# Attention memory of a fused attention and MLP-mixer kernel divided into pools by time of last use, and the main channel weights laid as a pool each on what falls free first

## The chip, the cores and the metric

The kernel runs on one core of a Trainium2 chip. The metric is the device time of one execution in microseconds (us); lower is better. TensorE (PE) does the matrix products, ScalarE (ACT) the exponentials, casts and copies, VectorE (DVE) the elementwise work, GpSimd (POOL) part of the subtractions, and SyncE (SP) issues all DMAs. Each of these takes its instructions in a fixed order.

## What is computed

Four batches, eight heads, 576 rows, head dimension 64. First linear attention with 256 exponential features, then two mixer blocks:

```python
def phi(x):
    proj = np.einsum('bhsd,df->bhsf', x, w_phi)
    proj = proj - np.max(np.abs(proj), axis=-1, keepdims=True)
    return np.concatenate([np.exp(proj), np.exp(-proj)], axis=-1)
kv = np.einsum('bhsf,bhsd->bhfd', k_p, v);  z = np.sum(k_p, axis=2)
num / (q_p . z + 1e-06)                     # attention
...
h = xt @ U @ V;  u = x + h.transpose(0, 2, 1)          # first block, rank 32 over the 576 tokens
u + np.maximum(u @ w_ch1, 0.0) @ w_ch2                 # 512 -> 2048 -> 512
...
h = np.maximum(xt @ w_tok1, 0.0) @ w_tok2;  u = x + h.transpose(0, 2, 1)   # second block, 576 -> 256 -> 576
u + np.maximum(u @ w_ch1, 0.0) @ w_ch2                 # 512 -> 1536 -> 512
```

The weights of the mixers are float64.

## The kernel before

**Products.** Every fp32 product is made of three products in the chip's rounded fp32 type: each operand is split into a high part (a cast) and a low part (value minus high part), and hi·hi, hi·lo and lo·hi are added in PSUM. So a tile of weights exists twice, as `wh` and `wl`.

**Stages.** Phase A is the attention, in 16 groups `g` of two heads, five rounds each, four groups for a batch. Into its rounds are woven, for each batch, the token mix of the first mixer (`tm0`, `tm1`, `tm2`: tiles `xp`, `xh`, `xl`, `rp`, `rh`, `rl`, `mp`) and the first 5 of the 16 column tiles of its channel MLP (`ma_u`, `ma_h`, `ma_y`: tiles `uha`, `hp_a`, `hha`, `hla`, `yp`). The "a" weights of these five live in the pool `wring`. Phase B does the other 11 column tiles, b0 to b10, and the token mix of the second mixer (`hp_b`, `hhb`, `hlb`, `yb`, `gp`). Phase C is the second channel MLP. The partial result of phase A goes to DRAM (`sD`, `uD`) and comes back in phase B (`x`, `ub`).

**Weights.** They come as raw float64 bits. `load64` brings half a tile, 512 KB, into a buffer `raw`. ACT makes `w` and `r` of it (lines 138, 139), DVE puts them together with two SCALAR_TENSOR_TENSOR (lines 141, 144; "the STTs"), then `wh` is cast on ACT and `wl` made on POOL. A tile has two halves, `_0` and `_1`: so `w_b1_0` is the first half of tile b1. There are two `raw` buffers in the pool `stage`, and in phase B three more in `rawx`. Which one a half gets is settled by a running count (`halves`) that isn't reset between the phases, and stands at 13 where phase B begins: so b0_0, b0_1 and b2_0 go to `rawx`, and b1_0, b1_1 to `stage`.

**Memory.** Pools `a1`, `a2`, `at2`, `ac` hold phase A. They are closed, and the pools of phase B (`wrB` for the seven tiles b0 to b6, then `rawx`, `bc`, `b2`) are laid on the same bytes; each tile there waits for the last use of the tiles that it lies on. b7 to b10 are in `wring` and wait for the "a" weights. PSUM likewise: `psy` takes banks 0 to 3, `psh` banks 4 and 5, `psg` banks 6 and 7, on the banks that `psk` (1), `psx` (5) and `psm` (2) had in phase A.

**Order.** The kernel is written as a list of rounds, but a scheduler with a time model then sets the order of instructions on each engine; `bufs`, pools and waits enter there. That order is fixed in the program. The end of phase A is one chain: numerators of group 15 are copied (`nd`), their denominators collected by DMA (`pk`), inverted, spread by two DMAs (`rD`, `rec`), multiplied (`xT`), and then the last batch's `tm0` to `ma_y` runs (all with the number 3: `xp3`, `rp3`, `hp_a3`, `yp3`).

Of the kernel before, what the change touches and what calls it, by code (L numbers as in the profile page):

```python
# [75 lines left out]
O_MA = 8  # L76
# [11 lines left out]
def body(ctx, tc, kq, vd, w_phi, U, V, wm1, wt1, wt2, wm2, out):  # L88
# [105 lines left out]
    warm = a1.tile([P, 512], F32R, tag="kvT", name="warm")  # L194
# [4 lines left out]
    wpr = a1.tile([P, F], F32, tag="wpr", name="wpr")  # L199
# [38 lines left out]
    def load(g):  # L238
        b, hp = g // NPAIR, g % NPAIR
        for i in range(NT):  # L240
            raws[g, i] = a1.tile([P, 2 * P], F32, tag="kq", name=f"kq{g}_{i}", bufs=KQB)
# [470 lines left out]
```

## Time and profile before

| | |
|---|---|
| median of three runs | 1089.06 us (1086.58 to 1089.66) |
| the profiled execution | 1084.32 us |
| its span, first to last instruction | 1082.5 us |
| around the span (difference) | 1.8 us |
| mean granted clock of TensorE in it | 0.984 |
| PE busy | 1038.5 us (96%) |
| DVE, ACT, POOL busy | 579.9, 420.0, 225.2 us |

Times in the views are microseconds from the start of the span. "Idle before, <- releaser" tells how long an engine stood before an instruction and which instruction ended that. TensorE's clock has two levels, 2.4 GHz (granted clock 1.00) and 1.2 GHz; a granted clock between is a mean over a stretch. Engines work in order, so an instruction that waits holds up all that stands behind it on its engine. Phase A ends and phase B begins at about 421 us.

### The profile page before, as it was taken

The page shows a single profiled execution, that of the slowest core. Times are in us where ns is not written, and L with a number is a line of the kernel's source. Part 1 is how long each engine was busy: PE and PEld are TensorE (multiplying, and loading weights), DVE is VectorE, ACT ScalarE, POOL GpSimd, SP SyncE. Part 2 cuts the span into 40 slices and gives each one's busy share as a digit, 9 for nine tenths or more (in the row PEclk, how much of TensorE's full clock was granted, in tenths as well). Part 3 has the DMA queues.
Part 4 walks back from the last instruction along what each step waited for, and adds up shares of the span by engine and source line. Part 5 has one row for each costly group of instructions (what it writes and reads, how often), then busy time and mean ns, then how long its engine had stood idle before and what let it go on. Part 6 is the DMA issues. An engine that isn't in the chain of part 4 may idle for free.

```text
span 1082.5 us, 16491 instructions
## 1 busy us (share of the span) xinstructions
PE 1038.5 (96%) x6528; PEld 945.5 (87%) x6528; DVE 579.9 (54%) x973; ACT 420.0 (39%) x953; POOL 225.2 (21%) x174
## 2 busy tenths in 40 slices
PE   8988999899989897999999999999999999999998
PEld 6767899799879797999999999999898888888886
DVE  7888988998898498733223223339941121211211
ACT  6766666755565466522112112137621111110110
POOL 3316566545555134100000000003200000000000
PEclk9988999999999889999999999999999999999999
DMA  7542322232221387520200200216401020020101
GB/s 214 169 139 63 98 73 75 72 96 71 80 74 45 109 287 228 168 79 22 88 23 22 88 22 23 88 41 208 143 23 61 1 77 1 1 77 1 39 1 38
DMA packets 59612, 87.36 MB, mean 81 GB/s; under 512 B 14352, under 2 KB 46352, under 8 KB 59536
## 3 DMA queue, kind: packets, MB, share of 16 engines
q1 hardware_dynamic: 59536, 86.32, 25.1%
q8 instruction: 51, 0.84, 0.3%
q14 instruction: 25, 0.20, 0.1%
HBM read 67.27 MB, written 18.95 MB: 80 GB/s over the span
## 4 chain that ended last, share of the span: by engine, by line
PE 78%; DVE 10%; ACT 4%; DMA 4%; issue 3%; POOL 1%; SPq 0%; DVEq 0%; ACTq 0%; POOLq 0%
PE hp_c L106 14%; PE yc L106 14%; PE hp_b L106 11%; PE yb L106 11%; PE hp_a L106 4%; PE pp L106 3%; PE yp L106 3%; PE nm L106 3%; PE kvp L106 3%; PE gp L106 3%; PE m2p L106 2%; PE dT L354 1%; DVE w_b L141 1%; DMA raw_b<-in_wm_dram 1%; DVE w_b L144 1%
## 5 line engine op out<-in xcount | busy, mean ns | idle before, releaser
L180 DVE SCALAR_TENSOR_TENSOR hlc<-hp_c,hhc 128x504 fp32r<-128x504 f32 (+1 forms) x60 | 38.2, 637 | 225.3 <-ACT hhc L179 225.3
L179 ACT ACTIVATE hhc<-hp_c 128x504 fp32r<-128x504 f32 (+1 forms) x60 | 33.4, 556 | 247.4 <-PE hp_c L106 247.4
L180 DVE SCALAR_TENSOR_TENSOR hlb<-hp_b,hhb 128x288 fp32r<-128x288 f32 x88 | 40.0, 456 | 157.9 <-ACT hhb L179 157.9
L179 ACT ACTIVATE hhb<-hp_b 128x288 fp32r<-128x288 f32 x88 | 36.0, 409 | 197.8 <-PE hp_b L106 197.5
L106 PE MATMUL hp_b<-uhb,wh_b 128*128 128x288 f32 x352 | 103.9, 296 | 3.4 <-DVE xT L491 3.4
L106 PE MATMUL hp_b<-ulb,wh_b 128*128 128x288 f32 x352 | 104.0, 296 | 0.0
L106 PE MATMUL hp_b<-uhb,wl_b 128*128 128x288 f32 x352 | 104.0, 296 | 0.0
L106 PE MATMUL yb<-hlb,wh_b 128*128 128x288 f32 x352 | 97.5, 297 | 1.4 <-DVE hlb L180 1.3
L106 PE MATMUL yb<-hhb,wl_b 128*128 128x288 f32 x352 | 97.1, 295 | 0.0
L106 PE MATMUL hp_c<-ulc,wh_c 128*128 128x504 f32 (+1 forms) x240 | 89.1, 371 | 0.0
L106 PE MATMUL hp_c<-uhc,wl_c 128*128 128x504 f32 (+1 forms) x240 | 89.1, 371 | 0.0
L106 PE MATMUL hp_c<-uhc,wh_c 128*128 128x504 f32 (+1 forms) x240 | 88.5, 371 | 0.0
L106 PE MATMUL yc<-hlc,wh_c 128*128 128x504 f32 (+1 forms) x240 | 88.3, 371 | 0.0
L106 PE MATMUL yc<-hhc,wl_c 128*128 128x504 f32 (+1 forms) x240 | 88.1, 370 | 0.0
L99 POOL TENSOR_TENSOR wl_c<-w_c,wh_c 128x512 fp32r<-128x512 f32 x12 | 19.1, 1593 | 326.6 <-ACT wh_c L94 312.5
L99 POOL TENSOR_TENSOR qel<-qe,qeh 128x640 fp32r<-128x640 f32 (+1 forms) x48 | 71.6, 1504 | 25.7 <-ACT qeh L94 10.7
L106 PE MATMUL yc<-hhc,wh_c 128*128 128x504 f32 (+1 forms) x240 | 75.7, 371 | 0.0
L106 PEld LDWEIGHTS hp_b<-uhb,wh_b 128*128 128x128 f32 x352 | 66.0, 188 | 4.9 <-DVE xT L491 3.6
L106 PE MATMUL yb<-hhb,wh_b 128*128 128x288 f32 x352 | 67.7, 296 | 0.9 <-ACT hhb L179 0.9
L106 PEld LDWEIGHTS yb<-hlb,wh_b 128*128 128x128 f32 x352 | 66.1, 188 | 2.5 <-DVE hlb L180 2.4
L106 PEld LDWEIGHTS hp_b<-ulb,wh_b 128*128 128x128 f32 x352 | 66.3, 188 | 0.1
L106 PEld LDWEIGHTS yb<-hhb,wl_b 128*128 128x128 f32 x352 | 66.2, 188 | 0.0
(181 smaller groups left out, 2796.4 us busy)
## 6 DMA issues: line engine op xcount, KB each, us to landing
raw_c<-in_wm_dram SPq DMA_DIRECT2D x24, 512.0 KB, 4.5
raw_b<-in_wm_dram SPq DMA_DIRECT2D x22, 512.0 KB, 4.7
kq<-in_kq_dram SPq DMA_DIRECT2D x80, 128.0 KB, 2.2
raw_a<-in_wm_dram SPq DMA_DIRECT2D x10, 512.0 KB, 4.0
rec<-rD SPq DMA_DIRECT2D x32, 144.0 KB, 3.2
uD<-xT SPq DMA_DIRECT2D x8, 576.0 KB, 3.4
sD<-xT SPq DMA_DIRECT2D x8, 576.0 KB, 5.3
x<-sD SPq DMA_DIRECT2D x8, 576.0 KB, 5.1
```

What stands on the lines that cost most here:

```text
L99: return ENG[e].tensor_tensor(out=o, in0=a, in1=b, op=ALU.subtract)
L106: nc.tensor.matmul(o, l, r, start=start, stop=stop, skip_group_check=True)
L141: nc.vector.scalar_tensor_tensor(out=wi, in0=wi, scalar=3, in1=r, op0=ALU.logical_shift_left, op1=ALU.bitwise_or)
L144: nc.vector.scalar_tensor_tensor(out=wi, in0=top, scalar=-(2**31), in1=wi, op0=ALU.bitwise_and, op1=ALU.bitwise_or)
L179: nc.scalar.activation(hh, hp, AF.Relu)
L180: nc.vector.scalar_tensor_tensor(out=hl, in0=hp, scalar=0.0, in1=f32(hh), op0=ALU.max, op1=ALU.subtract)
L354: nc.tensor.transpose(tp[:, o : o + r], ds["q", g, t][:r, j, :], ident[:r, :r])
```

## The change

The pools `a1` and `a2` become five: `ax` (projection weights, inputs and their splits), `ak` (features of k), `ad` (`kvT`, `km`, `kd`), `aq` (`KH`, `KL`, features of q) and `an` (`nd`, `pk`, `rec`). The tags and numbers of buffers stay. `wrB` becomes seven pools of one tile each, and `rawx` stands between the second and the third of them, so that the tiles of phase B lie on other tiles of phase A than before. The count in `load64` starts anew at phase B, so that b0_0 and b0_1 go to `stage` and b1_0, b1_1, b2_0 to `rawx`. `psh` is opened ahead of `psy`: `psh` gets banks 0 and 1, `psy` 2 to 5. `O_MA` becomes a tuple of four eights, which gives the same rounds. The number and kind of instructions on each engine is the same.

```diff
-O_MA = 8
+O_MA = (8, 8, 8, 8)
...
-    halves, extra = [], []
+    halves, extra = [0], []
...
-        pool = stage if len(halves) % (RAWB + RAWX) < RAWB or not extra else extra[0]
-        halves.append(name)
+        pool = stage if halves[0] % (RAWB + RAWX) < RAWB or not extra else extra[0]
+        halves[0] += 1
...
-        a1 = A.enter_context(tc.tile_pool(name="a1", bufs=1))
-        a2 = A.enter_context(tc.tile_pool(name="a2", bufs=2))
+        ax = A.enter_context(tc.tile_pool(name="ax", bufs=1))
+        ak = A.enter_context(tc.tile_pool(name="ak", bufs=1))
+        ad = A.enter_context(tc.tile_pool(name="ad", bufs=1))
+        aq = A.enter_context(tc.tile_pool(name="aq", bufs=2))
+        an = A.enter_context(tc.tile_pool(name="an", bufs=1))
...
-        e = a2.tile([P, 2, 2, F], F32, tag="ke", name=f"ke{g}_{t}", bufs=KEB)
+        e = ak.tile([P, 2, 2, F], F32, tag="ke", name=f"ke{g}_{t}", bufs=KEB)
...
-            nds[g, j] = a1.tile([P, S], F32, tag=f"nd{j}", name=f"nd{g}_{j}")
+            nds[g, j] = an.tile([P, S], F32, tag=f"nd{j}", name=f"nd{g}_{j}")
...
-        wrB = ctx.enter_context(tc.tile_pool(name="wrB", bufs=NR, reuse_waits="tile"))
-        extra.append(ctx.enter_context(tc.tile_pool(name="rawx", bufs=RAWX, reuse_waits="tile")))
+        wrB = []
+        for f in range(NR):
+            wrB.append(ctx.enter_context(tc.tile_pool(name=f"wrB{f}", bufs=1, reuse_waits="tile")))
+            if f == 1:
+                extra.append(ctx.enter_context(tc.tile_pool(name="rawx", bufs=RAWX, reuse_waits="tile")))
+    halves[0] = 0
...
+    psh = ctx.enter_context(tc.tile_pool(name="psh", bufs=2, space=PSUM, reuse_waits="tile"))
     psy = ctx.enter_context(tc.tile_pool(name="psy", bufs=1, space=PSUM, reuse_waits="tile"))
-    psh = ctx.enter_context(tc.tile_pool(name="psh", bufs=2, space=PSUM, reuse_waits="tile"))
...
-    wB = [load_w(wrB if f < NR else wring, wm1, NA + f, f"b{f}") for f in range(nB)]
+    wB = [load_w(wrB[f] if f < NR else wring, wm1, NA + f, f"b{f}") for f in range(nB)]
```

What moves is the order on ACT, DVE, POOL and SP. Four instructions of tile b0's first load go into group 4's work near 75 us; the loads and conversions of b1 to b7 begin in the last group, g = 15, and no more behind it; and the order on PE shifts a little between 85 and 215 us and between 340 and 432 us. In the rows below the last number of a name counts instructions, and the numbers ahead of it are those of the tile.

On ACT, near 75 us, before and then after: `nd3` are the numerators of group 3, `keh4` features of group 4.

```order
L94 CAST keh4_0_910<-ke4_0_907 128x512
L94 COPY nd3_0_850<-nm3_0_0_847 128x320
L94 COPY nd3_1_855<-nm3_1_0_852 128x320
L94 CAST xgh5_0_1067<-kq5_0_872 128x256
L94 COPY nd3_0_850<-nm3_0_1_884 128x256
```

```order
L94 CAST keh4_0_919<-ke4_0_916 128x512
L138 ACTIVATE w_b0_0_5588<-raw_b0_0_5586 128x512
L139 ACTIVATE r_b0_0_5589<-raw_b0_0_5586 128x512
L94 COPY nd3_0_859<-nm3_0_0_856 128x320
L94 COPY nd3_1_864<-nm3_1_0_861 128x320
L94 CAST xgh5_0_1076<-kq5_0_881 128x256
L94 COPY nd3_0_859<-nm3_0_1_893 128x256
L139 ACTIVATE r_b0_1_5599<-raw_b0_1_5596 128x512
L138 ACTIVATE w_b0_1_5598<-raw_b0_1_5596 128x512
```

The two pairs that make b0's `w` and `r` now stand in front of and between group 3's copies.

On ACT, at the end of the last group (the `qe15` and `nd15` are that group's features of q and numerators, `hha2` the third batch's hidden layer, `xh3` the first step of the last token mix), before:

```order
L94 COPY nd15_0_4830<-nm15_0_1_4860 128x256
L94 COPY nd15_1_4839<-nm15_1_1_4868 128x256
L179 ACTIVATE hha2_1_3_5085<-hp_a2_1_3_5072 128x288
L179 ACTIVATE hha2_1_4_5136<-hp_a2_1_4_5123 128x288
L138 ACTIVATE w_b0_0_5558<-raw_b0_0_5556 128x512
L139 ACTIVATE r_b0_0_5559<-raw_b0_0_5556 128x512
L94 CAST xh3_0_4967<-xp3_0_4962 128x512
L138 ACTIVATE w_b0_1_5568<-raw_b0_1_5566 128x512
```

and after, from the first of these conversions on:

```order
L138 ACTIVATE w_b1_0_5610<-raw_b1_0_5608 128x512
L139 ACTIVATE r_b1_0_5611<-raw_b1_0_5608 128x512
L363 ACTIVATE qe15_1_1_4825<-dT15_1_1_4822 128x256
L364 ACTIVATE qe15_1_1_4825<-dT15_1_1_4822 128x256
L94 CAST qeh15_0_1_4818<-qe15_0_1_4815 128x2x256
L138 ACTIVATE w_b1_1_5620<-raw_b1_1_5618 128x512
L139 ACTIVATE r_b1_1_5621<-raw_b1_1_5618 128x512
L179 ACTIVATE hha2_1_1_5045<-hp_a2_1_1_5032 128x288
...
L138 ACTIVATE w_b2_0_5632<-raw_b2_0_5630 128x512
L179 ACTIVATE hha2_1_3_5094<-hp_a2_1_3_5081 128x288
L94 COPY nd15_1_4848<-nm15_1_1_4877 128x256
```

Conversions of b1 and b2 now stand between the last group's features and its last copy; before, the first one came behind all of them.

On DVE, at the collecting of the denominators (`pk15`), before:

```order
L180 SCALAR_TENSOR_TENSOR hla2_1_3_5086<-hp_a2_1_3_5072,hha2_1_3_5085 128x288
L395 TENSOR_SCALAR pk15_4910<-pk15_4910 128x9
L396 RECIPROCAL pk15_4910<-pk15_4910 128x9
L180 SCALAR_TENSOR_TENSOR hla2_1_4_5137<-hp_a2_1_4_5123,hha2_1_4_5136 128x288
L491 TENSOR_TENSOR xT2_2880<-yp2_1_0_5140,xT2_2880 128x288
```

and after:

```order
L398 TENSOR_SCALAR pk15_4919<-pk15_4919 128x9
L180 SCALAR_TENSOR_TENSOR hla2_1_4_5146<-hp_a2_1_4_5132,hha2_1_4_5145 128x288
L144 SCALAR_TENSOR_TENSOR w_b2_1_5642<-raw_b2_1_5640,w_b2_1_5642 128x512
L399 RECIPROCAL pk15_4919<-pk15_4919 128x9
L494 TENSOR_TENSOR xT2_2889<-yp2_1_0_5149,xT2_2889 128x288
```

Between the sum and the reciprocal there are now two more instructions.

On SP, at the same place, after the change (before, all loads of b tiles stood behind the two `rec15`):

```order
L391 DMA pk15_4919<-nd15_0_4839 64x1x9
L392 DMA pk15_4919<-nd15_1_4848 64x1x9
L133 DMA raw_b4_1_5684<-in_wm1_dram 128x512
L133 DMA raw_b5_0_5696<-in_wm1_dram 128x512
L401 DMA rD15_4941<-pk15_4919 128x9
L403 DMA rec15_4943<-rD15_4941 64x576
L404 DMA rec15_4943<-rD15_4941 64x576
L133 DMA raw_b5_1_5706<-in_wm1_dram 128x512
```

Two loads of weights stand ahead of the spreading of the reciprocals.

On DVE, at the end of phase A, before: `hla3` and `yp3` belong to the last batch.

```order
L144 SCALAR_TENSOR_TENSOR w_b7_0_5712<-raw_b7_0_5710,w_b7_0_5712 128x512
L99 TENSOR_TENSOR ulb0_1_6228<-ub0_1_6225,uhb0_1_6227 128x1152
L491 TENSOR_TENSOR xT3_4303<-yp3_1_0_5456,xT3_4303 128x288
L141 SCALAR_TENSOR_TENSOR w_b7_1_5722<-w_b7_1_5722,r_b7_1_5723 128x512
L491 TENSOR_TENSOR xT3_4303<-yp3_1_1_5473,xT3_4303 128x288
L144 SCALAR_TENSOR_TENSOR w_b7_1_5722<-raw_b7_1_5720,w_b7_1_5722 128x512
L491 TENSOR_TENSOR xT3_4303<-yp3_1_2_5490,xT3_4303 128x288
L491 TENSOR_TENSOR xT3_4303<-yp3_1_3_5507,xT3_4303 128x288
```

and after:

```order
L180 SCALAR_TENSOR_TENSOR hla3_1_4_5462<-hp_a3_1_4_5448,hha3_1_4_5461 128x288
L99 TENSOR_TENSOR ulb0_1_6258<-ub0_1_6255,uhb0_1_6257 128x1152
L494 TENSOR_TENSOR xT3_4312<-yp3_1_0_5465,xT3_4312 128x288
L494 TENSOR_TENSOR xT3_4312<-yp3_1_1_5482,xT3_4312 128x288
L494 TENSOR_TENSOR xT3_4312<-yp3_1_2_5499,xT3_4312 128x288
L494 TENSOR_TENSOR xT3_4312<-yp3_1_3_5516,xT3_4312 128x288
```

The conversions are gone from this place; they stand further ahead.

## Rows read from the trace of the kernel before

**Rows 1.** The page's first section: engine, busy us, share of the span, instructions.

```profile
PE 1038.5 (96%) x6528; PEld 945.5 (87%) x6528; DVE 579.9 (54%) x973; ACT 420.0 (39%) x953; POOL 225.2 (21%) x174
```

**Rows 2.** Busy time by stretch: us, length, PE, PEld, DVE, ACT, POOL, clock, DMA share, GB/s.

```profile
360.00:380.00 20.00, 15.43 (x77) 12.57 (x76) 12.21 (x21) 10.85 (x20) 3.21 (x3) 0.79 0.46 155
380.00:400.00 20.00, 19.29 (x128) 18.60 (x128) 18.29 (x27) 13.82 (x24) 7.39 (x7) 0.87 0.94 319
420.00:440.00 20.00, 14.96 (x109) 14.26 (x108) 15.41 (x20) 12.58 (x24) 8.27 (x7) 1.00 0.62 196
440.00:460.00 20.00, 19.95 (x150) 19.68 (x149) 14.52 (x36) 9.37 (x24) 2.57 (x2) 1.00 0.56 165
```

**Rows 3.** Waits of PE from 360 to 440: who for whom, total us, times, longest.

```profile
PE hp_b L106 <- DVE xT L491: 3.4, 1, 3.4
PE rp L106 <- ACT xh L94: 3.2, 1, 3.2
PE yp L106 <- DVE hla L180: 1.2, 2, 0.9
PE yb L106 <- DVE hlb L180: 1.2, 1, 1.2
PE yb L106 <- ACT hhb L179: 0.5, 1, 0.5
```

**Rows 4.** Timeline of PE: start, length, instruction, [idle before and releaser].

```profile
369.45 0.80 PE L106 MATMUL rp<-xh,US 128*128 128x512 f32 x1 [3.16 <-ACT xh L94]
...
383.88 0.61 PE L106 MATMUL hp_a<-uha,wh_a 128*128 128x288 f32 x1 [0.47 <-ACT uha L94]
...
424.42 0.40 PE L106 MATMUL hp_b<-uhb,wh_b 128*128 128x288 f32 x1 [3.41 <-DVE xT L491]
```

**Rows 5.** Timeline of DVE at three places.

```profile
359.58 0.17 DVE L395 TENSOR_SCALAR pk<-pk 128x9 f32<-128x9 f32 x1 [0.46 <-DMA pk<-nd]
...
364.37 1.54 DVE L411 TENSOR_TENSOR xT<-nd,rec 64x576 f32<-64x576 f32 x2 [2.07 <-DMA rec<-rD]
...
379.42 1.76 DVE L144 SCALAR_TENSOR_TENSOR w_b<-raw_b,w_b 128x512 int32<-128x512 int32 x1
381.11 2.27 DVE L445 TENSOR_TENSOR xT<-mp,xT 128x288 f32<-128x288 f32 x6
```

**Rows 6.** Timeline of ACT at six places.

```profile
74.61 0.43 ACT L94 COPY nd<-nm 128x320 f32<-128x320 f32 x1 [0.86 <-PE nm L106]
...
346.27 0.59 ACT L94 COPY kvT<-kvp 128x512 f32<-128x512 f32 x1 [0.60 <-PE kvp L106]
...
350.55 0.40 ACT L360 ACTIVATE qe<-dT 128x256 f32<-128x256 f32 x1
...
357.30 0.37 ACT L94 COPY nd<-nm 128x256 f32<-128x256 f32 x1 [0.74 <-PE nm L106]
...
367.71 0.66 ACT L138 ACTIVATE w_b<-raw_b 128x512 f32<-128x512 f32 x1 [7.48 <-DMA raw_b<-in_wm_dram]
...
368.82 0.58 ACT L94 CAST xh<-xp 128x512 fp32r<-128x512 f32 x1
```

**Rows 7.** Timeline of SP, its DMA issues, at two places.

```profile
70.64 3.65 SPq L133 DMA_DIRECT2D raw_b<-in_wm_dram  x2
...
361.97 0.59 SPq L401 DMA_DIRECT2D rec<-rD  x1
362.67 8.57 SPq L133 DMA_DIRECT2D raw_b<-in_wm_dram  x4
```

**Rows 8.** The page's DMA issues: operation, count, size, median us to landing.

```profile
raw_b<-in_wm_dram SPq DMA_DIRECT2D x22, 512.0 KB, 4.7
```

**Rows 9.** The STTs on raw_b from 340 to 440 us: shortest, median, longest ns.

```profile
L144 DVE SCALAR_TENSOR_TENSOR w_b<-raw_b,w_b x21: 675/692/1761, 370.2 to 439.0; 128x512 int32<-128x512 int32 x21
```

**Rows 10.** Loads of kq, 128 KB each, from 60 to 90 us.

```profile
DMA to landing us min/median/max: 2.0/2.3/4.0
```

**Rows 11.** Busy time from 60 to 120 us, the sum of three stretches.

```profile
sum 60.00, PE 50.07 PEld 41.50 DVE 50.67 ACT 39.65 POOL 29.41; mean PE 16.69 PEld 13.83 DVE 16.89 ACT 13.22 POOL 9.80
```

More of the change, by code (lines that the diff above doesn't have):

```diff
@@ L192, in body @@
     psm = PS.enter_context(tc.tile_pool(name="psm", bufs=PSMB, space=PSUM))
-    warm = a1.tile([P, 512], F32R, tag="kvT", name="warm")
+    warm = ad.tile([P, 512], F32R, tag="kvT", name="warm")
     nc.vector.memset(f32(warm), 0.0)
@@ L198, in body @@
         mm(wp, warm[:, :P], warm, i == 0, i == WARM - 1)
-    wpr = a1.tile([P, F], F32, tag="wpr", name="wpr")
+    wpr = ax.tile([P, F], F32, tag="wpr", name="wpr")
     nc.sync.dma_start(wpr[0:D], w_phi)
@@ L240, in load @@
         for i in range(NT):
-            raws[g, i] = a1.tile([P, 2 * P], F32, tag="kq", name=f"kq{g}_{i}", bufs=KQB)
+            raws[g, i] = ax.tile([P, 2 * P], F32, tag="kq", name=f"kq{g}_{i}", bufs=KQB)
             nc.sync.dma_start(raws[g, i], kq[b, hp, :, i])
@@ L250, in load_v @@
         else:
-            vrs[g] = a1.tile([P, NT, 2, D], F32, tag="vr", name=f"vr{g}")
+            vrs[g] = ax.tile([P, NT, 2, D], F32, tag="vr", name=f"vr{g}")
             nc.sync.dma_start(vrs[g], vd[b, hp])
@@ L256, in g_split @@
             return
-        xh = a1.tile([P, 2 * P], F32R, tag="xgh", name=f"xgh{g}_{i}", bufs=XGB)
-        xl = a1.tile([P, 2 * P], F32R, tag="xgl", name=f"xgl{g}_{i}", bufs=XGB)
+        xh = ax.tile([P, 2 * P], F32R, tag="xgh", name=f"xgh{g}_{i}", bufs=XGB)
+        xl = ax.tile([P, 2 * P], F32R, tag="xgl", name=f"xgl{g}_{i}", bufs=XGB)
         split(raws[g, i], xh, xl, "a", "v")
@@ L300, in k1 @@
             return
-        eh = a2.tile([P, 2, 2 * F], F32R, tag="keh", name=f"keh{g}_{t}", bufs=KHB)
+        eh = ak.tile([P, 2, 2 * F], F32R, tag="keh", name=f"keh{g}_{t}", bufs=KHB)
         cp(KHI[t], eh, ev)
         if t < 4:
-            el = a2.tile([P, 2, 2 * F], F32R, tag="kel", name=f"kel{g}_{t}", bufs=KHB)
+            el = ak.tile([P, 2, 2 * F], F32R, tag="kel", name=f"kel{g}_{t}", bufs=KHB)
             sub(KLO[t], el, ev, f32(eh))
@@ L329, in k3 @@
     def k3(g):
-        kvT = a1.tile([P, 2, 2 * F], F32, tag="kvT", name=f"kvT{g}")
+        kvT = ad.tile([P, 2, 2 * F], F32, tag="kvT", name=f"kvT{g}")
         cp("a", kvT, kvps.pop(g))
@@ L364, in q1 @@
             return
-        eh = a2.tile([P, 2, 320], F32R, tag="qeh", name=f"qeh{nm}", bufs=QHB)[:, :, :n]
-        el = a2.tile([P, 2, 320], F32R, tag="qel", name=f"qel{nm}", bufs=QHB)[:, :, :n]
+        eh = aq.tile([P, 2, 320], F32R, tag="qeh", name=f"qeh{nm}", bufs=QHB)[:, :, :n]
+        el = aq.tile([P, 2, 320], F32R, tag="qel", name=f"qel{nm}", bufs=QHB)[:, :, :n]
         split(e, eh, el, QHI[2 * ch + j], "p")
@@ L386, in x0 @@
     def x0(g):
-        pk = a2.tile([P, 9], F32, tag="pk", name=f"pk{g}")
+        pk = an.tile([P, 9], F32, tag="pk", bufs=2, name=f"pk{g}")
         nc.sync.dma_start(pk[0:D], nds[g, 0][D : D + 1, :])
@@ L398, in xr @@
         nc.sync.dma_start(rD.rearrange("a (p i) -> (a p) i", i=9), pk)
-        rec = a1.tile([P, S], F32, tag="rec", name=f"rec{g}", bufs=RECB)
+        rec = an.tile([P, S], F32, tag="rec", name=f"rec{g}", bufs=RECB)
         nc.sync.dma_start(rec[0:D], rD[0:1].to_broadcast([D, S]))
@@ L640, in body @@
     BX.close()
-    wC = [load_w(wrB if f < NR else wring, wm2, f, f"c{f}") for f in range(NF2)]
+    wC = [load_w(wrB[f] if f < NR else wring, wm2, f, f"c{f}") for f in range(NF2)]
     with tc.using_default_side("right"):
```

16 lines of the change are left out of this document (8 added, 8 removed).

## The prediction

> **What bounds the kernel now.** I read the page's busy times first: PE is busy 96% of the span [rows 1], so only time in which PE stands still, or runs slowly, can be won. Next I read the busy times by stretch, to find where that is. The stretch 440 to 460 is what a full one looks like: 150 matmuls, clock 1.00. Around the seam of phases A and B it is otherwise: 77 matmuls from 360 to 380 at clock 0.79, 128 from 380 to 400, 109 from 420 to 440 [rows 2]. Then the waits of PE in that region, which name the releasers: 3.4 us at the first `hp_b`, 3.2 us at `rp`, 1.2 at `yp`, 1.2 and 0.5 at `yb` [rows 3], 9.5 us together. The other loss there is the low clock on a chain of small steps, `rp3` (369.45) to `hp_a3` (383.88), 14.4 us long [rows 4]. The timelines tell why PE waits. DVE is busy 18.29 of 20 us from 380 to 400 [rows 2], and much of that are the STTs that put the weights b1 to b7 together. On ACT, `xh3` runs at 368.82 only, because a `w_b` stands ahead of it and waits for its DMA until 367.71 [rows 6]; that DMA was issued at 362.67, behind the last `rec` [rows 7].
>
> So the seam is where the change can act. It puts no instruction on PE and takes none away.
>
> **The change part by part.** The sum is made against the profiled execution, 1084.32 us (span 1082.5 and 1.8 around it). That one is 4.7 us under the median of 1089.06, so I carry the difference over to the median.
>
> *Two halves of b0 early, near 75 us.* The load that stood there, issued at 70.64 [rows 7], becomes b0's, and ACT now stands for it ahead of the copies of group 3. With the median of 4.7 us [rows 8] it lands at 75.3. ACT had nothing to do from 73.75 (74.61 less 0.86, [rows 6]). Two conversions of 0.66 [rows 6] follow, so the first copy ends its wait at 76.6 in place of 74.6, 2.0 us late. DVE gets four STTs of 0.69 to 1.76 [rows 9], 2.8 to 7 us. But of the 60 us around, DVE is busy 50.67 and PE 50.07 [rows 11]: neither is full, and group 3's copies are several rounds ahead of their use in `xT`. Ends: -1 (PE's order from 85 to 215 us moves a little, and may move well) and +4 (the 2.0 us and half of four slow STTs come through). I take +0.5, near zero, as both engines have air.
>
> *The seam, first part: the weights in the last group's way.* The loads of b1 may now start once the last features of k are used by the `kvp` products, whose copy began at 346.27 [rows 6]. An estimate from that row and from the median landing of 4.7 us [rows 8] puts the first load's landing at 351.3, with 0.3 for the issue. On ACT its two conversions, 1.3 us, stand ahead of a feature step that began at 350.55 [rows 6]: 2.0 us late. The next two conversions and a cast, ahead of the hidden layer and the last copies, add about 1.0 net: I take 3.0 us for the last copy of `nd15`, which began at 357.30 [rows 6]. Bounds 2.6 and 3.6. Behind this wait stand the casts of `qeh15` and the steps of `hha2`, and behind those PE's products; but these have the gap at 366 to run into, so only the chain to `xT3` counts. Next, between the sum of `pk15` (359.58, [rows 5]) and its reciprocal stand an `hla2` of 0.46 and an STT of 0.69 to 1.76 [rows 9]: 1.1 us, bounds 0.7 and 2.2. Next, `rD15` stands on SP behind two loads of 512 KB. The nearest row is `kq` behind a load, 4.0 us at most against 2.3 in the median [rows 10]: 1.7 us. Bounds 0, if the loads have gone, and 3.3, which is 1.05 MB at the 319 GB/s of the busiest stretch [rows 2]. So the `xT3` products, which ended at 365.91 (364.37 and 1.54, [rows 5]), come 5.8 us later.
>
> The Trainium skill (DMA: Bandwidth & Descriptors, section "Queues, rings and completion order") says that each DMA engine takes the descriptors of a queue in ring order, so that a small transfer waits for all bytes queued ahead of it. By that rule the upper bound of 3.3 holds and the sum comes out 1.6 us higher; the `kq` row agrees that it costs something, and no row here has a tiny transfer behind two loads.
>
> *The seam, second part: what is no more in the way.* With those products done, `xh3` needs no DMA any more: by the durations on PE and ACT it would have let `rp3` start at about 367.35, some 1.4 us behind `xT3` (four transposes of about 0.2 and a cast of 0.58, [rows 6]), and not at 369.45 [rows 4]. That is 2.1 us back. In the chain behind, an STT of 1.76 at 379.42 stands ahead of the sums into `xT3` at 381.11 [rows 5]; after the change none stands there: 1.6 us back. Other conversions, of b4 to b7, stand between the same steps, as b0 to b2 did; I count no difference. So `hp_a3` comes at 5.8 - 2.1 - 1.6 = +2.1 us. Bounds: 2.6 + 0.7 + 0 - 3.7 = -0.4 and 3.6 + 2.2 + 3.3 - 2.1 = +7.0.
>
> *The seam, third part: the waits up to 430 us.* From `hp_a3` to the first products of b0, DVE no longer has conversions between its steps. The two waits of `yp` for `hla` go: -1.2. The first `hp_b` waited 3.4 us for the last sum into `xT` [rows 3, 4], since its PSUM bank held the `yp3` of that sum. Its bank is now one that was free 70 us before, its weights b0 are made near 80 us, and its inputs are ready before `yp3` ends: -3.4. The wait of `yb` for `hlb`, 1.2, came from STTs of b8 and b9 ahead of it [rows 3]. The four of b8 stand there still, but their inputs are ready, so they run while PE does the first `hp_b`: -1.2. Of ACT's 0.5 I count a half. Together -6.0. Bounds -6.3 (all five rows but `rp`) and -4.6 (the first and the `hla` alone). What cover do these have? If b8 to b10 came late, PE would wait there again. At 150 matmuls in 20 us [rows 2] the 24 of a tile take 3.2 us, so PE reaches b10 some 32 us after the first `hp_b`, at 424.42 [rows 4]; the last of the 21 STTs listed began at 439.0 [rows 9], 14.6 us after it. There is room.
>
> *No cost:* the five pools of phase A hold the same tags with the same buffers; `O_MA` gives the same rounds; phase C has the same pools under other names.
>
> The sum: 0.5 + 2.1 - 6.0 = -3.4 us. On the profiled execution that is 1080.9, on the median 1085.6.
>
> **The rivals.** *A, the tail is held longer, and the kernel gets slower.* The chain from the first wait on ACT to `xT3` is made of three in-order queues, ACT, DVE and SP, each with a load or a conversion put ahead of the critical step. At its upper bounds (+7.0), with the early halves at +2 and the savings at -4.6, the result is +4.4: 1093.5. The point from which the change loses is `hp_a3` 5.5 us late, which is `xT3` about 9 us late, at 375. For it: everything on that chain is short, and a load in flight is long (4.7 us); the clock is low there anyway (0.79, [rows 2]), and more idle time won't raise it. Against it: the loads come in spread out by DVE's pace, not four at once. The ring rule above is part of this rival.
>
> *B, the tail isn't held.* The loads land before ACT needs them, and the last copies come less than a microsecond late. Then `hp_a3` comes 2 to 3 us earlier rather than later, and the waits go as well: 0 - 2.5 - 6.0 = -8.5, 1080.6. For it: at 360 to 380 the DMA engines are busy less than half of the time [rows 2]. Against it: 350.55 is only 4.3 us after the earliest issue that I see, and a load takes 4.7.
>
> *C, a new wait takes the place of the old at the seam.* b7 to b10 lie in `wring` and wait for `yp3` as before. If PE, starting 3.4 us earlier, caught up with them, the gain at `hp_b` would come back as a wait for `wh_b`; with the tail at +2.1 that is -3.4 + 3.4 = 0, 1089. Against it: the room of 17 us worked out above. That the change doesn't do what it says, in that the loads aren't earlier at all, I leave out: they stand earlier in the order and what they wait for ends earlier.
>
> **How the numbers follow.** About 0.3%, 3.3 us, is what a measurement of this kernel can tell from no change: 1085.8 to 1092.3 is "the same". My forecast (0.58) is -3.4, give or take 4, just about on that edge: half of it is faster, nearly half the same. B has 0.15 and is faster. A has 0.18, all but a little slower. C has 0.09, the same. That gives faster 0.44, same 0.37, slower 0.19. The range of 8 in 10 goes from 1079.5, a little beyond B, to 1093, nearly the price of A.
>
> **What would show it.** In the profile of the changed kernel: the wait of PE at the first `hp_b` gone and `hp_b` directly behind `yp3`; no waits of `yp` for `hla` from 400 on; ACT idle for a DMA at about 347 to 352 ahead of `w_b`; the `xT3` products ending near 372 and `hp_a3` starting near 386. I am wrong if the `xT3` products come beyond 375 (A), if they come at 367 or sooner (B), if PE waits for a `wh_b` of b7 to b10 (C), or if PE's waits from 60 to 220 us change by more than 4 us, which no step here accounts for.

## The result: slower by 0.7%

| | median | span of the runs | runs |
|---|---|---|---|
| before | 1087.30 us | 1081.27 to 1089.66 | 6 |
| changed | 1092.43 us | 1088.52 to 1096.46 | 6 |

The ratio is 1.0072 (95% interval 1.0051 to 1.0094), where 0.997 was forecast. (Three of the six runs of before are those that the prediction started from. Against the median of the other three, 1084.95 us, the changed kernel's median is 0.7% longer; against that of all six, 0.5%.) In a later set of runs on one chip (e11 below) the changed kernel stood at 1.0060 (1.0039 to 1.0080). The profiled execution of the changed kernel took 1091.15 us, with a span of 1089.4: 6.9 us over that of before.

**Where the time went.** I matched instructions by their names in the two programs and compared the start or end of the same one in both traces. "Late" means against the profiled execution of before.

| point in the program | before | changed | late |
|---|---|---|---|
| last `kvp` product of group 3 | 66.37 | 68.29 | +1.9 |
| last `kvp` product of group 10 | 225.28 | 233.86 | +8.6 |
| last `kvp` product of group 14 | 321.14 | 329.75 | +8.6 |
| first `rp3` | 369.45 | 383.53 | +14.1 |
| first `hp_a3` | 383.88 | 398.57 | +14.7 |
| last `yp3` | 421.01 | 433.44 | +12.4 |
| last product of the first `yb` | 463.84 | 470.74 | +6.9 |
| last product | 1077.88 | 1085.01 | +7.1 |

So there are three pieces. The attention loses 6.7 us between 66 and 225 us (the 1.9 ahead of that arise where no engine's order has changed). The way to `hp_a3` loses another 6.1. From there to the end of the first `yb` 7.8 come back. The seam as a whole gains 1.7, and the early part loses four times that.

The waits of PE around the seam in the changed kernel: who waited for whom, total, times, longest.

```profile
PE xp L426 <- DVE xT L414: 6.3, 1, 6.3
PE rp L106 <- DVE xl L99: 1.2, 2, 1.0
PE hp_a L106 <- ACT uha L94: 1.1, 1, 1.1
PE mp L106 <- DVE rl L99: 0.9, 1, 0.9
PE mp L106 <- ACT rh L94: 0.7, 1, 0.7
PE yp L106 <- DVE hla L180: 0.7, 1, 0.7
PE rp L106 <- ACT xh L94: 0.7, 1, 0.7
...
PE yb L106 <- ACT hhb L179: 0.2, 1, 0.2
```

Against [rows 3] the 3.4 us at `hp_b` are gone, and so are those of `yp3` and of `yb` for `hlb`. The 3.2 us of `rp` for `xh` have become 0.7. But ahead of it stands a new wait, 6.3 us of `xp3` for the `xT3` products. (The 0.7 of `yp` for `hla` is at 370 us, in the third batch.)

The busy time by stretch, columns as in [rows 2]:

```profile
360.00:380.00 20.00, 15.34 (x114) 14.87 (x113) 15.46 (x25) 15.65 (x32) 10.40 (x8) 1.00 0.57 185
380.00:400.00 20.00, 12.99 (x54) 9.96 (x54) 18.17 (x28) 13.69 (x24) 7.09 (x5) 0.74 0.62 209
400.00:420.00 20.00, 19.73 (x148) 19.36 (x147) 13.16 (x19) 7.78 (x14) 2.90 (x2) 1.00 0.70 236
420.00:440.00 20.00, 19.75 (x147) 19.40 (x147) 9.77 (x16) 9.15 (x17) 5.50 (x4) 1.00 0.46 148
```

The stretch of the token mix is now 380 to 400, with 54 matmuls and a clock of 0.74; behind it PE is full, 148 and 147 matmuls, and DVE has air (13.16 and 9.77 of 20 us). That is what the change was laid out for; it stands behind a longer hole.

**The early piece.** On ACT at 75 us, in the changed kernel (start, length, instruction, idle before):

```profile
75.06 0.64 ACT L94 CAST keh<-ke 128x512 fp32r<-128x512 f32 x1
77.36 0.67 ACT L138 ACTIVATE w_b<-raw_b 128x512 f32<-128x512 f32 x1 [1.66 <-DMA raw_b<-in_wm_dram]
77.93 0.66 ACT L139 ACTIVATE r_b<-raw_b 128x512 int32<-128x512 uint32 x1
78.49 0.74 ACT L94 COPY nd<-nm 128x320 f32<-128x320 f32 x2
```

ACT stood 1.66 us for the load, as forecast, and the two copies of `nd3` came behind it. Both halves of b0 are converted here, with four instructions on ACT and four STTs on DVE, and once they are read two more loads of 512 KB go out, from 83.18 us on. (Up to 140 us no engine waits for a load of `kq`, which stands behind these two.) The busy time from 80 to 90 us of the changed kernel, and then that of the same work in before, which stands 1.9 us earlier there:

```profile
80.00:90.00 10.00, 7.52 (x52) 6.50 (x51) 10.00 (x15) 5.85 (x16) 3.14 (x3) 1.00 0.48 138
```

```profile
78.08:88.08 10.00, 8.49 (x58) 7.28 (x58) 8.63 (x15) 6.10 (x18) 4.43 (x4) 1.00 0.19 50
```

DVE had 1.37 us of air in these ten; with four STTs in or near them it has none, and what PE waits for there stands behind them. The waits of PE in the changed kernel from 75 to 93 us:

```profile
85.68 0.51 PE L106 MATMUL kvp<-keh,va 128*128 128x256 f32 x2 [0.52 <-ACT keh L94]
87.03 0.50 PE L106 MATMUL kvp<-kel,va 128*128 128x256 f32 x2 [0.62 <-POOL kel L99]
89.33 1.53 PE L357 MATMUL dT<-ident,kd 128*128 128x128 f32 x6 [1.34 <-DVE kd L99]
92.04 0.80 PE L106 MATMUL kvp<-keh,va 128*128 128x256 f32 x2 [0.45 <-POOL keh L99]
```

In before the same products, from 73 to 89 us, have one wait:

```profile
87.82 0.50 PE L106 MATMUL kvp<-keh,va 128*128 128x256 f32 x2 [1.51 <-POOL keh L99]
```

PE's own order differs from before too, from 81.9 us on, and by more than the "little" of the section on the change: between the last `kvp` products of groups 3 and 8, PE does 30 more matmuls than before, all of them `yp` of the first batch's MLP, and between those of groups 8 and 9 it does 30 fewer of these.

**The seam.** On ACT (the last copy of `nd15`), DVE and SP in the changed kernel, at the denominators of the last group:

```profile
368.47 0.36 ACT L94 COPY nd<-nm 128x256 f32<-128x256 f32 x1
```

```profile
370.86 0.16 DVE L398 TENSOR_SCALAR pk<-pk 128x9 f32<-128x9 f32 x1
370.94 0.44 DVE L180 SCALAR_TENSOR_TENSOR hla<-hp_a,hha 128x288 fp32r<-128x288 f32 x1
371.31 1.60 DVE L144 SCALAR_TENSOR_TENSOR w_b<-raw_b,w_b 128x512 int32<-128x512 int32 x1
372.83 0.20 DVE L399 RECIPROCAL pk<-pk 128x9 f32<-128x9 f32 x1
...
379.83 0.75 DVE L414 TENSOR_TENSOR xT<-nd,rec 64x576 f32<-64x576 f32 x1 [0.70 <-DMA rec<-rD]
381.23 1.09 DVE L414 TENSOR_TENSOR xT<-nd,rec 64x576 f32<-64x576 f32 x1 [0.65 <-DMA rec<-rD]
```

```profile
370.37 2.95 SPq L133 DMA_DIRECT2D raw_b<-in_wm_dram  x2
373.42 0.37 SPq L401 DMA_DIRECT2D rD<-pk  x1
376.78 0.46 SPq L403 DMA_DIRECT2D rec<-rD  x1
377.29 0.59 SPq L404 DMA_DIRECT2D rec<-rD  x1
```

and in before, on DVE and SP:

```profile
359.79 0.22 DVE L396 RECIPROCAL pk<-pk 128x9 f32<-128x9 f32 x1
```

```profile
360.03 0.33 SPq L398 DMA_DIRECT2D rD<-pk  x1
361.46 0.46 SPq L400 DMA_DIRECT2D rec<-rD  x1
```

From the sum of `pk` to the reciprocal it is 1.97 us where it was 0.21 (359.58, [rows 5], to 359.79). `rD` is issued at 373.42 and the first `rec`, which waits for it, at 376.78: 3.36 us, where it was 1.43.

### The profile page after: what moved, and what is told of

It reads as the page before. It is cut to its first block, busy times and chain, and to the rows that moved or that the text cites. A ratio compares the mean times of both kernels' runs of the same rounds, so it can differ in the third digit from the quotient of the medians.

```text
span 1089.4 us, 16500 instructions
## 1 busy us (share of the span) xinstructions
PE 1039.3 (95%) x6528; PEld 944.6 (87%) x6528; DVE 580.1 (53%) x973; ACT 419.6 (39%) x953; POOL 227.0 (21%) x174
## 4 chain that ended last, share of the span: by engine, by line
PE 77%; DVE 12%; DMA 4%; ACT 3%; issue 2%; POOL 0%; SPq 0%; DVEq 0%; ACTq 0%; POOLq 0%
PE hp_c L106 14%; PE yc L106 14%; PE yb L106 12%; PE hp_b L106 12%; PE yp L106 5%; PE hp_a L106 5%; PE pp L106 3%; PE gp L106 3%; PE kvp L106 2%; PE m2p L106 2%; PE nm L106 2%; DVE xT L414 2%; DVE km L289 1%; DMA raw_a<-in_wm_dram 1%; DMA rec<-rD 1%
## 5 line engine op out<-in xcount | busy, mean ns | idle before, releaser
L106 PEld LDWEIGHTS yb<-hhb,wl_b 128*128 128x128 f32 x352 | 66.2, 188 | 0.0
```

The costliest lines, as they stand in the source:

```text
L106: nc.tensor.matmul(o, l, r, start=start, stop=stop, skip_group_check=True)
```

## The experiments

Each ran in five rounds beside the kernel before; the ratio is against the runs of before in the same set, the stretches are from one profile of each kernel. The table puts all side by side; the stretches are cut at instructions that all kernels have, so that chance in the first 66 us (where all have the same order, and the profiled executions differ by up to 4.6 us) doesn't enter. In e11, the changed kernel again, I had expected 7 to 8 us to come back behind `hp_a3`; it was 6.2.

| kernel | ratio (95%) | 66 to 225: `kvp` of group 3 to that of 10 | `kvp` of group 14 to `hp_a3` | `hp_a3` to the end of the first `yb` |
|---|---|---|---|---|
| before | 1 | 158.9 us | 62.7 us | 80.0 us |
| changed | 1.0072 (1.0051 to 1.0094) | 165.6 | 68.8 | 72.2 |
| e11 changed, again | 1.0060 (1.0039 to 1.0080) | 166.8 | 68.7 | 73.8 |
| e1 banks only | 1.0024 (1.0008 to 1.0039) | 158.8 | 63.0 | 82.9 |
| e2 count anew only | 1.0019 (1.0004 to 1.0033) | 165.1 | 61.7 | 76.8 |
| e3 changed, count not anew | 1.0021 (1.0007 to 1.0036) | 158.5 | 73.6 | 73.0 |
| e4 divided pools only | 1.0019 (1.0003 to 1.0036) | 156.9 | 73.6 | 73.1 |
| e5 b0 held to group 15 | 0.9979 (0.9965 to 0.9992) | 158.9 | 68.6 | 72.5 |
| e6 b0 held to group 8 | 1.0032 (1.0016 to 1.0048) | 160.1 | 71.9 | 71.5 |
| e9 b0 held to group 4 | 1.0044 (1.0023 to 1.0066) | 160.9 | 71.6 | 74.2 |
| e12 MLP order pinned | 1.0134 (1.0107 to 1.0161) | 166.4 | 71.8 | 76.2 |
| e10 loads behind `rec15` | 1.0052 (1.0035 to 1.0069) | 162.2 | 68.6 | 73.8 |
| e7 seam held, count not anew | 0.9960 (0.9944 to 0.9976) | 157.6 | 62.0 | 74.7 |
| e8 seam held, count anew | 0.9929 (0.9910 to 0.9948) | 155.6 | 62.0 | 74.9 |

Two theories on the loss. Theory 1: the early conversions of b0 make it, between 70 and 225 us. Theory 2: conversions and loads in the chain of the last group make it. They are not exclusive.

### The parts of the change alone: e1 to e4

e1 swaps the two lines that open `psh` and `psy`; no instruction changes its place.

```diff
+    psh = ctx.enter_context(tc.tile_pool(name="psh", bufs=2, space=PSUM, reuse_waits="tile"))
     psy = ctx.enter_context(tc.tile_pool(name="psy", bufs=1, space=PSUM, reuse_waits="tile"))
-    psh = ctx.enter_context(tc.tile_pool(name="psh", bufs=2, space=PSUM, reuse_waits="tile"))
```

Expected:

> The kernel before with only the pool psh opened ahead of psy: no instruction changes its place on any engine, only the banks differ. If the wait of PE at the first hp_b is the bank's (theory 1), that wait of 3.4 us goes, PE starts hp_b0 right behind yp3, and the time falls by about 3 us (ratio 0.997); the STTs of b8 then stand in the way at hlb, so that up to 1 us may come back. If the wait is really for weights or inputs (rival), the wait stays at 3 us or more under another name and the ratio is 1.000.

The waits of PE in e1 behind the last `yp3` (timeline of PE, rows with idle time):

```profile
429.50 1.33 PE L106 MATMUL yb<-hhb,wh_b 128*128 128x288 f32 x4 [4.12 <-ACT hhb L179]
431.47 0.61 PE L106 MATMUL yb<-hlb,wh_b 128*128 128x288 f32 x1 [0.64 <-DVE hlb L180]
```

The wait at `hp_b` is gone, so it was the bank's; but its time stands again 7 us later, as 4.12 us of `yb` for `hhb`. From the last `yp3` to the first `yb` it is 7.33 us in both (421.01 to 428.34, 422.17 to 429.50). ACT and DVE, with b7 and b8 to convert, set the first `yb`; whether PE waits in one place or two is no matter. Expected was -3 us, or nothing; it came out 0.24% slower. In e1 the clock from 420 to 440 is 0.83 against 1.00 [rows 2]; I didn't test whether the single longer wait brings that.

e2 starts the count anew, and nothing else (the count itself is written as in the change):

```diff
...
+    halves[0] = 0
     BX = ExitStack()
```

Expected:

> The kernel before with only the count of halves started anew at phase B: b0's first two halves are loaded and converted near 75 us, as in the changed kernel, and the weights' pools stay as they were. Theory 1 (the early conversions and the order that the scheduler makes behind them cost the changed kernel its time): by 220 us the work is 4 to 7 us late against the kernel before, ratio about 1.004 to 1.006. Rival (the loss in the first 220 us was chance, and the late end comes from the last group): by 220 us within 2 us of before, ratio at most 1.001, since at the seam b0's conversions are gone.

From 66 to 225 it takes 165.1 us where before takes 158.9: theory 1 holds, 6.2 us. The seven kernels of the table with before's order in this stretch (before, e1, e3, e4, e5, e7, e8) take 157.9 in the mean, from 155.6 to 158.9; the four with the changed kernel's (changed, e11, e2, e10) 164.9, from 162.2 to 166.8. So the price is 7.0 us, and one profile is good to some 2. The ratio is lower than I expected for it, since at the seam 4.2 come back (61.7 + 76.8 against 62.7 + 80.0). I read that as the conversions of b0 that the seam no longer has to make, so that part of the early loss is a loan; no run tests it.

e3 is the changed kernel without that line:

```diff
-    halves[0] = 0
```

> The changed kernel without the new start of the count: the pools are divided and psh lies first, the early conversions near 75 us are not there, and the order up to 340 us is that of before. Theory 1: the work at 220 us is as in before (within 2 us); at the seam hp_a3 comes 4 to 6 us late and the waits behind it are gone, net -1 to -3; ratio about 0.998. Rival (the last group's held tail is what makes the changed kernel slower): ratio 1.004 or more.

The early stretch is as before, 158.5, as theory 1 has it. But the seam isn't -1 to -3: `hp_a3` comes 10.9 us late and only 7.0 come back. So theory 2 holds as well, and more strongly where b0 is converted there too. I had expected 4 to 6 us and a ratio of 0.998; it is 1.0021, between that and the rival's 1.004.

e4 is e3 with `psh` behind `psy` as in before:

> As the run without the new start of the count, but psh behind psy as in before: the divided pools alone. Theory 1: hp_a3 4 to 6 us late; the first hp_b waits for the last sum into xT, though with no conversions ahead of that sum only about 1 us; ratio 0.999 to 1.001. Rival (tail): 1.005 or more.

The same within 1 us at the seam (73.6 and 73.1 against 73.6 and 73.0), with a ratio of 1.0019, again above what I expected. The first `hp_b` waits 0.6 us for the last sum into `xT`, where before it was 3.4 with the same banks. The banks matter as little with the divided pools as without them.

### Where the early conversions may stand: e5, e6, e9, e12

All three of e5, e6 and e9 are the changed kernel, with the conversions of the b tiles queued on ACT behind the copy of `kvT` of one group: 15, 8 or 4. The edit of e6 (in e9 `HG` is 4; e5 holds them behind the last copy, that of group 15):

```diff
+HG = 8
...
-        cp("a", kvT, kvps.pop(g))
+        hold[g] = nc.scalar.copy(kvT, kvps.pop(g)).ins
...
-    wB = [load_w(wrB[f] if f < NR else wring, wm1, NA + f, f"b{f}") for f in range(nB)]
+    with tc.issue_after(hold[HG]):
+        wB = [load_w(wrB[f] if f < NR else wring, wm1, NA + f, f"b{f}") for f in range(nB)]
```

> The changed kernel, with the weights' conversions on ACT queued behind the copy of kvT15 (about 346 us); b0's loads still stand near 75 us. The order up to 340 us is that of before but for these loads. If the four early conversions make the 6 to 7 us (theory 1a), the work at 220 us is within 1.5 us of before; if the loads or where the pools lie make them (rival), it stays 4 us or more late. The last group is held as in the changed kernel or more, hp_a3 6 to 11 us late, and the waits behind it are gone (-7 to -8): ratio 0.998 to 1.003.

158.9 us from 66 to 225, the same as before: the early loss comes with the conversions (and with the order that the scheduler makes behind them, see e9), not with b0's loads or the pools. The kernel is 0.2% faster than before and 0.9% under the ratio of the changed one, though its `hp_a3` is as late (68.6).

> The changed kernel, with the same four conversions of b0 queued behind the copy of kvT8 (about 178 us), where PE has no waits and the data landed 100 us before. If the cost belongs to the place (theory 1b: from 70 to 120 us PE waits for ACT and DVE, and ACT waits for the landing of the load), it costs 0 to 2 us here by 220 us. If the engine time of the conversions costs wherever they stand (rival), 4 us or more. The seam as in the changed kernel: net -1 to -2. Ratio 0.998 to 1.001.

160.1 us: the four conversions at 180 us, on data that landed long ago, cost 2.2 us against that mean, just beyond the upper end of what I expected, and not 7.0 as at 77 us. The seam (71.9 and 71.5) isn't as good as in the changed kernel, on an order of its own, and the ratio of 1.0032 missed the 0.998 to 1.001 that I had expected.

> The changed kernel, with the four conversions of b0 on ACT queued behind the copy of kvT4 (about 89 us): their data has landed 8 us before, so ACT waits for no DMA there, but they stay in the stretch in which PE waits for ACT and DVE. If ACT's wait for the landing makes most of the early loss, 0 to 3 us are lost by 220 us. If the stretch itself makes it, 5 us or more. Ratio 1.001 to 1.007 accordingly.

At 94 us, behind the landing but in the stretch in which PE waits for ACT and DVE, they cost 3.0 (160.9), within the 0 to 3 us that I had put down for ACT's wait. It looks as if more than half of the early loss belonged to the place ahead of `nd3`, with the wait for the load. The traces say otherwise. Here is the busy time cut at the last `kvp` products of groups 3, 6 and 9, columns as in [rows 2], of before, of the changed kernel and of e9. Between these cuts every kernel has nearly the same products on PE.

```profile
66.37:132.32 65.95, 56.08 (x344) 49.61 (x344) 56.05 (x97) 42.47 (x112) 33.41 (x25) 0.87 0.31 95
132.32:200.91 68.59, 67.95 (x526) 66.08 (x526) 58.41 (x99) 44.05 (x119) 38.57 (x30) 1.00 0.26 74
```

```profile
68.29:137.96 69.67, 57.26 (x346) 49.39 (x345) 61.40 (x101) 44.65 (x116) 32.87 (x25) 0.88 0.35 106
137.96:209.70 71.74, 69.24 (x528) 66.61 (x527) 60.35 (x99) 43.54 (x119) 39.46 (x30) 1.00 0.25 71
```

```profile
70.78:138.53 67.75, 55.47 (x345) 48.08 (x344) 58.62 (x100) 44.99 (x116) 33.56 (x25) 0.90 0.35 107
138.53:207.31 68.78, 68.06 (x525) 66.21 (x526) 58.23 (x100) 43.79 (x119) 38.53 (x30) 1.00 0.26 75
```

From group 3 to group 6, where the conversions stand, the four kernels with the changed kernel's order take 68.1 us in the mean (66.4 to 69.7) and the seven with that of before 64.8 (62.4 to 66.0). So the conversions cost 3.3 us directly at 77 us, and 2.9 at 94 (e9): the wait for the landing adds nothing that can be told from chance. From group 6 to group 9 no conversion stands in any of the three kernels above, and the clock is 1.00 in all. Yet the changed kernel takes 3.1 us longer, and e9 0.2. What differs there is the order: e9 and the seven, all with PE's order of before, take 68.6 to 68.8, and the four, with the 30 `yp` taken ahead, 71.7 to 74.6 (two of them, e2 and e11, also have a clock below 1.00 there). PE waits 2.5 us in this stretch of the changed kernel, for `keh`, `kel`, `kd` and `xT`, and 0.6 in before. So the early loss has two parts of like size: the conversions themselves, and what I put down to the order of the work that comes with them. In the means they are 3.3 and 4.1 us, and 0.3 comes back from group 9 to 10. The ratio, 1.0044, is near that of the changed kernel all the same: the seam of e9 came out worse (71.6 against 68.8), on another order.

The last product of group 4's `kvp` comes 2.7 us later after that of group 3 than in before (24.97 and 22.26 us). How that becomes 7 by 225 I tried to settle with e12, before I had cut the traces as above. In the changed kernel the scheduler takes the first batch's MLP ahead of the products of groups 7 and 8; I thought that PE then lacked that filling work at 190 to 230 us.

```diff
-        group(yp[:, :N], gr)
+        if (b, ch) == (0, 1):
+            g = max(k for k in kvi if k <= (8, 4))
+            with tc.issue_after(kvi[g]):
+                group(yp[:, :N], gr)
+        else:
+            group(yp[:, :N], gr)
```

(and likewise for the last hidden tile of each half.)

> The changed kernel with b0's early conversions where they are, but PE's order in the first batch's MLP brought back near that of before: the last hidden tiles and the sums yp0 of that batch are queued behind the products kvp7 and kvp8, so that they are not taken ahead of the attention. If the early loss is made up of a direct delay and of this order, which takes PE's filling work early and leaves it waiting at 190 to 230 us (theory 1c), the work at 220 us is 2 to 5 us late and not 7 to 12, ratio 1.000 to 1.004. If the order has no part in it (rival), it stays 7 us or more late, ratio 1.005 to 1.009.

The stretch still takes 166.4 us, as the rival has it, and the order came out bad at the seam as well (71.8 and 76.2): the ratio of 1.0134 is above both ranges. But theory 1c doesn't fall by it, because the order of before wasn't brought back. Between the last `kvp` products of groups 6, 7, 8 and 9, PE does 177, 177 and 170 matmuls in before, 196, 188 and 141 in the changed kernel, and 168, 198 and 158 in e12; its waits from group 6 to 9 are 0.6, 2.5 and 3.3 us. So e12 put a third order in the place of the second. That the order costs some 3 us at the full clock follows from the comparison above alone: no run has the conversions at 77 us and the order of before behind them. Which of its moves costs the time stays open.

### The chain of the last group: e10, e7, e8

e10 moves on SP the loads of b4_1 and b5_0, and those behind them, from ahead of `rD15` to behind `rec15`. PE's order is unchanged. `hold["s"]` is the second `rec15`:

```diff
+            if name[0] == "b" and name not in ("b0_0", "b0_1", "b1_0", "b1_1", "b2_0", "b2_1", "b3_0", "b3_1", "b4_0"):
+                with tc.issue_after(hold["s"]):
+                    nc.sync.dma_start(raw[i * rows : (i + 1) * rows], src)
...
```

> The changed kernel, with one thing moved: on SP the loads of b4_1 and b5_0 and the later ones stand behind rec15 and not ahead of rD15; PE's order is the same. If the small rD15 waited for the bytes of the loads queued ahead of it, rD15 lands 1.4 to 1.6 us after its issue and not 3.3, and the xT3 products end 2 to 3 us earlier with respect to the reciprocal; hp_a3 1 to 3 us earlier than in the changed kernel, as some conversions come later. If DVE's order alone held it, rD15 still lands 3 us after its issue. The early loss of 6 to 7 us stays; ratio 1.003 to 1.007.

SP in e10, and the landing times of its `rD` and two `rec`, then those of the same three in the changed kernel:

```profile
372.21 0.33 SPq L405 DMA_DIRECT2D rD<-pk  x1
374.09 0.46 SPq L407 DMA_DIRECT2D rec<-rD  x1
374.59 0.59 SPq L408 DMA_DIRECT2D rec<-rD  x1
375.23 1.53 SPq L135 DMA_DIRECT2D raw_b<-in_wm_dram  x3
```

```profile
DMA to landing us min/median/max: 1.9/2.9/3.2
```

```profile
DMA to landing us min/median/max: 3.0/3.3/3.9
```

`rec` is issued 1.88 us after `rD` and not 3.36, and lands faster. So the loads ahead did hold the small transfers: 1.5 us on `rD` and the rest on `rec`. The `xT3` products end 8.1 us behind the start of the reciprocal and not 9.5: 1.4 us are gained, where I had expected 2 to 3. And `hp_a3` gained only 0.2 us (68.6 against 68.8): the time went to the conversions that stand between the steps behind. One wait taken out of the chain isn't enough.

e7 and e8 free the whole chain. On ACT the conversions of all b tiles stand behind the last copy of `nd15`, on DVE behind the reciprocal of `pk15`, and the loads but b0, b1 and b2_0 behind `rec15`. e7 doesn't start the count anew, e8 does.

```diff
-        cp("a", nds[g, j][:, QS[ch]], ps[:, :n])
+        hold["a"] = nc.scalar.copy(nds[g, j][:, QS[ch]], ps[:, :n]).ins
...
-        nc.vector.reciprocal(pk, pk)
+        hold["v"] = nc.vector.reciprocal(pk, pk).ins
...
+    with tc.issue_after(hold["a"]), tc.issue_after(hold["v"]):
         wB = [load_w(wrB[f] if f < NR else wring, wm1, NA + f, f"b{f}") for f in range(nB)]
```

> The changed kernel without the new start of the count, and with the weights' conversions held out of the chain of the last group: on ACT behind the last copy of nd15, on DVE behind the reciprocal of pk15, and on SP all loads but b0, b1 and b2_0 behind rec15. So the weights are converted while the denominators travel. If the late xT3 of the changed kernel comes from these conversions and loads in the chain (theory 2), xT3 ends within 2 us of before, hp_a3 comes 0 to 3 us earlier than before, and the waits behind it are gone: -5 to -8, ratio 0.993 to 0.996. If it comes from elsewhere (rival: the time of the copies or the clock), xT3 stays 4 us or more late.

> As the run before this one, with the count started anew, so that b0's loads land near 75 us and b1's and b2_0's in the last group; all conversions are held out of the chain. Theory 2 and theory 1a together: nothing lost by 220 us, hp_a3 0 to 3 us earlier, ratio 0.992 to 0.996.

Both did what was expected: `hp_a3` 0.7 us earlier, 5 us less behind it, and nothing lost early. Theory 2 holds. e8 is the fastest of all, 0.9929 (0.9910 to 0.9948), 1076.14 us against 1083.79 in the same set. Of its gain some 5.8 us are the seam; the 3.3 us in the early stretch, whose order is that of before but for b0's loads in the place of b1's, go with the clock: from group 3 to group 6 e8 takes 62.4 us at a granted clock of 0.95, before 66.0 at 0.87. I take that for chance, as other kernels with that order lie between 156.9 and 158.9 and b0's loads are in e5 as well. ACT and DVE in e8, at the denominators:

```profile
355.01 0.37 ACT L389 COPY nd<-nm 128x256 f32<-128x256 f32 x1 [0.74 <-PE nm L106]
355.28 0.67 ACT L142 ACTIVATE w_b<-raw_b 128x512 f32<-128x512 f32 x1
355.85 0.65 ACT L143 ACTIVATE r_b<-raw_b 128x512 int32<-128x512 uint32 x1
...
357.49 0.21 DVE L403 RECIPROCAL pk<-pk 128x9 f32<-128x9 f32 x1
357.62 1.23 DVE L145 SCALAR_TENSOR_TENSOR w_b<-w_b,r_b 128x512 int32<-128x512 int32 x2
...
362.01 2.59 DVE L418 TENSOR_TENSOR xT<-nd,rec 64x576 f32<-64x576 f32 x2 [1.22 <-DMA rec<-rD]
```

The last copy of `nd15` goes first, the conversions follow at once, in the seven microseconds in which the denominators travel, where ACT in before had stood idle for 7.48 us [rows 6], and `xT3` still waits for `rec` alone. Thus the memory that the divided pools free early is of use; what undid it was the place of the work on each engine.

## Why the prediction was wrong

The forecast was -3.4 us, made up of +0.5, +2.1 and -6.0. Measured against the same profile it was +6.7, +6.1 and -7.8.

**The early halves: the step that failed.** I put +0.5, with bounds -1 and +4; it is 7.0 in the mean of four kernels, 6.7 in this profile. ACT's wait was foreseen and came (1.66 us). Two things were wrong. The first is the argument for air, "neither is full", taken from a mean over 60 us (50.67 and 50.07). In the ten microseconds where the STTs stand, DVE had 1.37 us free and needs 3.8 for them (1.76, 0.68, 0.68, 0.68). And the second argument, that group 3's copies are needed rounds later, looked at the copies alone: the features of k of group 4 stand behind the same wait and the same STTs, and PE waits for those at once. This part costs some 3.3 us, inside the bounds. The second is PE's order, which I said "moves a little, and may move well": I let it gain 1 us and gave it no price the other way, without a row for either. From group 6 to group 9, with that order and no conversion, the changed kernel loses 3.1 us at the full clock, and the four kernels 4.1 in the mean. The two parts together are beyond the +4. The sign that I had named for this, PE's waits from 60 to 220 us changing by more than 4 us, is there when the traces are cut at the same work: from the last `kvp` of group 3 to that of group 10 PE waits 13.4 us before and 17.9 in the changed kernel (in the fixed window, which holds less of the late kernel's work, 13.1 and 16.2).

**The way to `hp_a3`.** Forecast +2.1 with bounds -0.4 and +7.0; measured +6.1 (68.8 against 62.7). By terms, each against the lateness of 8.6 that came from ahead:

| term | forecast | measured |
|---|---|---|
| last copy of `nd15` | +3.0 | +2.6 |
| sum of `pk` to reciprocal, and the hold ahead of it | +1.1 | +1.9 |
| `rD` and `rec` | +1.7 | +3.4 |
| `xT3` products, in all | +5.8 | +7.8 |
| `xh3` no more behind a load | -2.1 | -2.3 |
| chain `rp3` to `hp_a3` | -1.6 | +0.6 |

The mechanism of each was right but for the last; two were sized too low. For `rD` I took the middle, from the row of `kq`, and that was near: from `rD` to `rec` it is 3.36 us against 1.43, 1.9 more and not the 3.3 of the upper bound. The other 1.4 of this term I hadn't counted: `rD` is issued 0.35 us later behind the reciprocal, and from `rec` to the end of the `xT3` products it takes 1.1 us more. The rule of the Trainium skill (DMA: Bandwidth & Descriptors, section "Queues, rings and completion order"), that a queue's descriptors are taken in ring order, agrees with the changed trace and with e10, where `rec` follows `rD` 1.5 us sooner once no load is issued just ahead of them. That a small transfer therefore waits for all bytes queued ahead was my own conclusion from the rule, and it is too strong here: by the estimate in the prediction, two loads of 512 KB would have cost 3.3 us. The chain behind `rp3` didn't get shorter: I had counted the STT that goes and set the others "no difference", but the conversions of b4 to b7 stand there, where b0 to b2 stood, and PE now waits 1.2 us there for `xl` and 1.1 for `uha`; before, it was 0.2 for `xl` and 0.47 for `uha` [rows 4].

**The waits up to 430 us.** Forecast -6.0 with bounds -6.3 and -4.6; measured -7.8, and -6.2 in e11. The three waits are gone as forecast; by PE's waits alone the stretch gives -5.2 (6.8 us before, 1.6 after), and the rest of the 7.8 I hadn't counted. But the reason that I gave for the largest was wrong: e1 shows that the bank alone gives nothing, since the conversions on ACT and DVE hold the first `yb` anyhow, and e4 shows that the early weights give it without the bank (73.1 us against 73.0 in e3). The errors of this term and the one ahead of it, -1.8 and +4.0, partly cancel; that the seam as a whole still gains is luck.

**Rival A** named the right side but the wrong place: its price came from the seam, and the seam gained in the changed kernel (-1.7 and -0.2 in e11). In e3 and e4, without the early conversions, it is A as I wrote it, with 3.9 us lost at the seam. B and C aren't seen: no wait for `wh_b` appears, and the copies of `nd15` are late.

## What to carry to other kernels

Memory that falls free earlier lets a scheduler move work earlier, and on engines that work in order "earlier" means ahead of something: look at what stands behind each moved instruction, not at whether the engine has air in the mean. Look as well at the order that the scheduler then makes of everything else: here a stretch in which no moved instruction stands lost as much as the one in which they stand. A load or conversion for the next phase belongs behind the last step of the chain that ends this one (here the last copy, the reciprocal, the spreading DMAs), where it fills the time in which that chain travels. And when a wait is taken away by another bank or buffer alone, look at what would be waited for next: in e1 the whole wait came back at the next product.

## What the runs showed that I had not expected

Up to the end of group 3's `kvp` all kernels have the same order on every engine, and yet the profiled executions reach it between 66.2 us (e1) and 70.8 (e9). The spread goes with the clock: the six that reach it last, at 67.7 us or later, have a granted clock of 0.95 to 0.97 in the first 66 us, the other eight 1.00. One pair of profiles of this kernel can't tell less than some 4 us; stretches cut at the same instructions, and several rounds, can.

Swapping two pools of banks without moving an instruction made the kernel 0.24% slower (e1, 1.0008 to 1.0039), with a clock of 0.83 from 420 to 440 where it was 1.00 before.
